# Efficient attention and a mixture of depths on one core: k and v loaded by swapped halves of partitions, their fifth rows multiplied in quarters, the last choice of tokens moved forward, the last product halved, and q of two more units turned on VectorE

## The chip, the cores and the metric

The kernel runs on one core of one Trainium2 chip. A time is the device time of one execution in microseconds (us). A core has TensorE (matrix products, PE in the profile, with its weight loads as PEld), VectorE (DVE), ScalarE (ACT), GpSimd (POOL), SyncE (SP, which issues DMAs), and 16 DMA engines.

## The reference

```python
def _attn_ref(q, k, v):                       # 8 batches, 8 heads, 576 tokens, 64 wide, f32
    q_s = exp(q - max over d);  q_s = q_s / (sum over d + 1e-09)
    k_s = exp(k - max over s);  k_s = k_s / (sum over s + 1e-09)
    kv = np.einsum('bhsd,bhse->bhde', k_s, v)
    return np.einsum('bhsd,bhde->bhse', q_s, kv)

def _moe_ref(x, w_gate, w1, w2, capacity):    # x: (8, 576, 512), capacity 128
    scores = np.einsum('bsd,d->bs', x, w_gate)
    out = x.copy()
    for b in range(B):
        top_idx = np.argpartition(-scores[b], capacity)[:capacity]
        xe = x[b, top_idx]
        ye = np.maximum(xe @ w1, 0.0) @ w2    # w1: 512 x 1024, w2: 1024 x 512
        g = 1.0 / (1.0 + np.exp(-scores[b, top_idx]))
        out[b, top_idx] = x[b, top_idx] + g[:, None] * ye
    return out
```

The attention's heads, side by side, are the x of the second part.

## The kernel before

**Units and steps.** The attention is cut into 16 units of four heads, two units to a batch. A loop over steps `s` (from 3) works on unit `s`, prepares unit `s+1`, loads unit `s+3`, and beside it does one half of the dense products of batch `(s-3)//2`: `mlp1` (x by w1, L591, eight pieces) in odd steps, `mlp2` (by w2, L601, eight pieces) in even ones. The first three units are written out ahead of the loop. The order of instructions on each engine is the order in the text; every engine takes its own in that order and waits by semaphores. `pieces(n)` says how many pieces of the dense products are put at a place.

**A unit.** k, v and q each have three buffers in SBUF, taken in turn. `k_exp` and `v_copy` (ScalarE) make exp(k) and a copy of v with a column of ones. `kv_mm(u)` multiplies them into one PSUM tile `kv`; `kv_out` (DVE) divides by the sums. `q_exp` makes exp(q); `q_t` transposes it on TensorE (L384) and copies it back with ScalarE. For the units in `TWICE`, q is instead loaded in a doubled form of four DMAs, and `q_blocks` transposes it with two DVE instructions (L359). `x_mm` (L414, L405) multiplies q by kv, `x_sums` and `x_scale` (DVE) scale it, `x_store` writes it to `out`.

**Rows of k and v.** A head's 576 tokens are nine rows for each of 64 groups. Two partitions share a group's nine rows: of partitions 2j and 2j+1 the even one holds five rows, the odd one four, for all four heads. `kv_mm` sums five products over 128 partitions. In the fifth the odd partitions hold nothing: k and v are cleared there ahead of the first load of each buffer (`clear`), and the ones column of v is 0 there (`even`, `fifth`). A load is two DMAs, one for the odd partitions (256 elements for each of four heads) and one for the even ones (320).

**Choice of tokens.** After a batch's second unit (odd step), `score` adds up the scores, `score_row` transposes them on TensorE into the `kv` PSUM tile and ScalarE copies them out (`srow`), `compare` counts ranks (five DVE instructions, L493) and `hits` marks which token takes which slot. In the next step `find` turns that into indices (TensorE, L520), `fetch` gathers the rows of `out` (GpSimd, L534), and a step later `turn` transposes them (L571) for `mlp1`. After `mlp2`, `finish` adds gate times product to the rows (DVE, L614) and `put` scatters them (GpSimd, L606). Batch 0's result is kept (`finish_gated`) and written near the end.

**Queues.** SP issues in each step: the store of unit `s`, then k, v and q of unit `s+3`; it takes them in order. The units in `SPREAD` have half of their q issued by GpSimd, early in the step (`odd=True`). From unit 8 on each load's DMA waits for the landing of the one `DEEP` before it.

A fallback for inputs out of range (`general`) follows at the end and isn't entered.

Of the kernel before, what the change touches and what calls it, by code (L numbers as in the profile page):

```python
# [17 lines left out]
def kernel(  # L18
# [23 lines left out]
    nc = tc.nc  # L42
# [58 lines left out]
    LD = 3  # L101
    FLAT = 0, 1
    TWICE = (9, 11, 13, 14, 15)
    SPREAD = TWICE
    RR = 4 * R
# [58 lines left out]
    way = []  # L164
    DEEP = 4
    ROWS = (0, R), (R, T)
# [4 lines left out]

    def clear(u):
        for what in "kv":
            nc.gpsimd.memset(view(raw[what][u % LD], True)[:, :, N2], 0.0)

# [40 lines left out]
    nc.vector.tensor_scalar(valid, second_half, -1.0, 1.0, op0=OP.mult, op1=OP.add)  # L216
    even_p = const.tile([P, 1], I32, name="even_p")
    nc.gpsimd.iota(even_p, pattern=[[0, 1]], base=1, channel_multiplier=1)
    nc.vector.tensor_single_scalar(even_p, even_p, 1, op=OP.bitwise_and)
    even = const.tile([P, 1], F32, name="even")  # L220
    nc.vector.tensor_copy(out=even, in_=even_p)
    beyond = const.tile([P, 1], F32, name="beyond")
# [27 lines left out]
    nc.gpsimd.iota(whole.rearrange("p (b r) -> p b r", b=B), pattern=[[S, B], [1, R]], base=0, channel_multiplier=T)  # L250
    clear(2)
    dma_k = load(1, "k", flat=True)
# [39 lines left out]
    def q_exp(u, c):  # L292
        if c == 0:
            st["qe", u] = at.tile([P, T, 2, D], F32, tag="qe", name="qe")
        if u in TWICE and u not in FLAT:
            half = raw["q"][u % LD].rearrange("p (a n) (h s) -> p a n h s", a=2, h=2)[:, c, :, 0]
            to = st["qe", u].rearrange("p r i d -> p (r i d)").rearrange("p (a n s) -> p a n s", a=2, n=2 * T)
            nc.scalar.activation(out=to[:, c], in_=half, func=AF.Exp)
            return
        r0, r1 = ROWS[c]  # L300
        qr = raw["q"][u % LD][:, :2 * T].rearrange("p (i r) d -> p r i d", i=2)
        nc.scalar.activation(out=st["qe", u][:, r0:r1], in_=qr[:, r0:r1], func=AF.Exp)  # L302

    def v_copy(u, engine=nc.scalar):
# [3 lines left out]
        else:  # L308
            engine.tensor_copy(out=out_v, in_=in_v)

    def fifth(u):
        nc.gpsimd.tensor_copy(out=view(v_ones[u % 2], True)[:, :, N2, D:], in_=even[:, None].to_broadcast([P, 4, 1]))

    def kv_mm(u, crossed=False):
# [16 lines left out]
        for a in range(0 if u in FLAT else 2):  # L333
            for r in range(R):
                for i in range(2):
                    nc.tensor.matmul(out=kv_ps[part(i), a, :D + 1], lhsT=ke[:, 2 * i + a, r], rhs=vo[:, 2 * i + a, r],  # L336
                                     start=(r == 0), stop=(r == N2))
        st["kv", u] = [(slice(0, P), kv_ps[:, :, :D + 1])]
# [54 lines left out]
    def x_mm(u, a, wide=False, tag="x"):  # L393
# [5 lines left out]
        for r in range(R):  # L399
            for i, c in QUARTERS:  # L400
                to = x[part(c), i, r * C:(r + 1) * C]
                if r == N2:
                    if a == 0:
                        rows = by_token[part(i), c, r] if u in TWICE and u not in FLAT else qT[part(i), c, r, 0]
                        last = nc.tensor.matmul(out=to, lhsT=rows, rhs=kw[part(i), c], start=True, stop=True)  # L405
                    continue
                if wide:
# [4 lines left out]
                    continue  # L412
                rows = by_token[part(i), a, R * c + r] if u in TWICE and u not in FLAT else qT[part(i), a, r, c]
                last = nc.tensor.matmul(out=to, lhsT=rows, rhs=kw[part(i), a], start=True, stop=True)  # L414
# [189 lines left out]
    def put(b, n, o):  # L604
# [3 lines left out]
            in_=o[:m], in_offset=None)  # L608

    def finish(b, n):  # L610
        m = slots[n][1]
# [46 lines left out]
    def general():  # L658
        nonlocal FLAT
        FLAT = tuple(range(NU))  # L660
        for n in range(2):
            nc.gpsimd.memset(v_ones[n][:, :, D:], 1.0)
        for b in range(B):
# [79 lines left out]
    x_out(0, 0)  # L743
    clear(3)
    load(3, "kv")
# [10 lines left out]
    x_mm(1, 1)  # L756
    fifth(2)
    x_out(0, 1)
# [11 lines left out]
    q_t(2, 0, wide=True, later=True)  # L770
    clear(4)
    load(4, "kv")
# [13 lines left out]
    k_exp(3)  # L786
    fifth(3)
# [182 lines left out]
```

## Time and profile before

| | |
|---|---|
| median of 3 runs | 208.74 us (208.12 to 213.29) |
| the profiled execution | 209.41 us; its span, first to last instruction, 207.6 us |
| mean granted TensorE clock | 0.986 |
| busy: PE, DVE, ACT, POOL | 193.1, 127.0, 92.1, 40.9 us |
| L591, `mlp1` on PE | 512 instances, 61.8 us |
| L601, `mlp2` on PE | 128 instances, 58.4 us |
| L414, `x_mm` on PE | 960 instances, 22.0 us |
| L336, `kv_mm` on PE | 560 instances, 19.4 us |
| L384, `q_t` on PE | 144 instances, 6.4 us |
| moved by DMA | 49.43 MB, mean 238 GB/s |

An f32 product is listed as two instances, so 20 products are x40. "x" counts instances. A window's DMA share is the mean busy share of the 16 DMA engines; it can exceed 1 where packets overlap. The chain of waits follows back from the last instruction to what released each step; "DMA" in it is the time from an issue to its landing.

### The profile page before, as it was taken

The numbers are of one execution on the slowest core, as the hardware profiler recorded it, in microseconds if no ns is written. First come the engines' busy times: TensorE is split into PE (matmuls) and PEld (weight loads), VectorE is DVE, ScalarE is ACT, GpSimd is POOL, SyncE is SP. The second block draws the span as 40 slices with busy tenths as digits, with TensorE's granted clock in tenths as the row PEclk, the third lists the DMA queues.
The fourth block names the chain that finished last, engine by engine and source line by source line (L and its number), as shares of the span: only waits on it lengthen the run. The fifth ranks groups of instructions, "written<-read, shape, count | busy, mean of one in ns | idle before, by whom it ended". The sixth has DMA issues, their size and how long they took to land.

```text
span 207.6 us, 6693 instructions
## 1 busy us (share of the span) xinstructions
PE 193.1 (93%) x2801; PEld 146.1 (70%) x2801; DVE 127.0 (61%) x392; ACT 92.1 (44%) x136; POOL 40.9 (20%) x110
## 2 busy tenths in 40 slices
PE   7988899999999999999999999999999999999940
PEld 3576788885698749974897569864896479459510
DVE  5776935897278636957684948766696766432010
ACT  4475877673655814772347516452364012111100
POOL 7302100202020403140222132040402030224010
PEclk9999999999999999999999999999999999999995
DMA  6999999999699999899999899999970434031101
GB/s 219 396 294 344 376 363 371 372 374 351 152 295 285 289 356 381 215 296 261 251 285 280 255 230 262 308 269 233 338 210 18 95 114 114 1 102 54 58 17 41
DMA packets 36599, 49.43 MB, mean 238 GB/s; under 512 B 2513, under 2 KB 30673, under 8 KB 36562
## 3 DMA queue, kind: packets, MB, share of 16 engines
q1 hardware_dynamic: 34336, 41.57, 64.8%
q0 software_dynamic: 2080, 7.06, 11.5%
q8 instruction: 24, 0.39, 0.8%
q10 hardware_dynamic: 146, 0.30, 0.5%
q14 instruction: 13, 0.11, 0.1%
HBM read 37.39 MB, written 11.53 MB: 236 GB/s over the span
## 4 chain that ended last, share of the span: by engine, by line
PE 68%; DMA 21%; DVE 2%; issue 2%; ACT 2%; SPq 1%; POOL 1%; POOLq 0%; ACTq 0%
PE mm L591 22%; PE mm L601 21%; DMA k<-in_k_dram 11%; PE x L414 7%; PE kv L336 6%; DMA xr<-out_dram,idx 6%; DMA out_dram<-xs 4%; PE mm L204 3%; PE x L384 2%; PE mm L571 2%; PE kv L479 1%; PE kv L331 1%; PE x L405 1%; PE x L377 1%; DVE xs L439 1%
## 5 line engine op out<-in xcount | busy, mean ns | idle before, releaser
L591 PE MATMUL mm<-xT,w 128*128 128x128 f32 x512 | 61.8, 278 | 0.5 <-DVE xT L579 0.3
L591 PEld LDWEIGHTS mm<-xT,w 128*128 128x128 f32 x512 | 58.7, 192 | 2.3 <-ACT xT L579 1.0
L601 PE MATMUL mm<-w,hT 128*128 128x512 f32 x128 | 58.4, 599 | 0.0
L601 PEld LDWEIGHTS mm<-w,hT 128*128 128x128 f32 x128 | 23.0, 190 | 23.5 <-issue 23.0
L493 DVE SCALAR_TENSOR_TENSOR junk<-srow,s,not_before 128x576 bf16<-128x576 f32 x40 | 32.7, 818 | 5.2 <-ACT srow L485 4.1
L289 ACT ACTIVATE ke<-k 128x1280 f32<-128x1280 f32 (+1 forms) x16 | 20.2, 1260 | 9.8 <-DMA k<-in_k_dram 9.8
L414 PE MATMUL x<-kv_w,qT 64*64 64x66 f32 x960 | 22.0, 222 | 2.1 <-issue 1.4
L439 DVE TENSOR_TENSOR xs<-x,qrec 128x640 f32<-128x640 f32 (+1 forms) x31 | 23.5, 757 | 0.6 <-issue 0.3
L414 PEld LDWEIGHTS x<-kv_w,qT 64*64 64x64 f32 x960 | 18.7, 133 | 5.2 <-issue 4.3
L307 ACT COPY v_ones<-v 128x1280 f32<-128x1280 f32 x14 | 17.6, 1259 | 6.2 <-DMA v<-in_v_dram 6.2
L336 PEld LDWEIGHTS kv<-v_ones,ke 128*64 128x64 f32 x560 | 17.5, 137 | 3.4 <-issue 2.4
L336 PE MATMUL kv<-v_ones,ke 128*64 128x65 f32 x560 | 19.4, 224 | 0.2 <-ACT srow L485 0.2
L614 DVE SCALAR_TENSOR_TENSOR o<-mm,g,xr 128x512 f32<-128x512 f32 x7 | 5.3, 751 | 23.2 <-PE mm L601 23.2
L534 POOL DMA_INDIRECT xr<-out_dram,idx x8 | 8.5, 1061 | 54.6 <-DVE no L526 15.2
L579 ACT COPY xT<-mm 128x512 f32<-128x512 f32 x7 | 4.1, 585 | 31.5 <-PE mm L571 31.5
L606 POOL DMA_INDIRECT out_dram<-o,idx x7 | 7.2, 1026 | 50.5 <-DVE o L614 43.1
L594 ACT ACTIVATE hT<-mm 128x512 f32<-128x512 f32 x16 | 9.5, 596 | 16.5 <-PE mm L591 16.4
L302 ACT ACTIVATE qe<-q 128x640 f32<-128x640 f32 (+1 forms) x22 | 13.9, 677 | 3.5 <-DMA q<-in_q_dram 3.5
L391 ACT COPY qT<-x 128x640 f32<-128x640 f32 (+1 forms) x18 | 10.8, 648 | 9.0 <-PE x L384 8.2
L345 DVE RECIPROCAL krec<-kv 128x2 f32<-128x2 f32 x16 | 2.7, 170 | 18.8 <-PE kv L336 16.4
L431 DVE RECIPROCAL qrec<-x 128x10 f32<-128x10 f32 (+1 forms) x31 | 6.6, 213 | 9.4 <-PE x L405 7.6
L485 ACT ACTIVATE srow<-kv 128x576 f32<-128x576 f32 x7 | 4.5, 648 | 15.2 <-PE kv L479 15.2
(120 smaller groups left out, 187.3 us busy)
## 6 DMA issues: line engine op xcount, KB each, us to landing
out_dram<-xs SPq DMA_DIRECT2D x16, 320.0 KB
k<-in_k_dram SPq DMA_DIRECT2D x14, 320.0 KB
v<-in_v_dram SPq DMA_DIRECT2D x14, 320.0 KB
w<-in_moe_w_dram SPq DMA_DIRECT2D x8, 512.0 KB
out_dram<-xs SPq DMA_DIRECT2D x16, 256.0 KB
k<-in_k_dram SPq DMA_DIRECT2D x14, 256.0 KB
v<-in_v_dram SPq DMA_DIRECT2D x14, 256.0 KB
q<-in_q_dram SPq DMA_DIRECT2D x9, 320.0 KB
```

Source lines behind the costliest of these rows:

```text
L289: nc.scalar.activation(out=ke, in_=view(raw["k"][u % LD], u not in FLAT), func=AF.Exp)
L302: nc.scalar.activation(out=st["qe", u][:, r0:r1], in_=qr[:, r0:r1], func=AF.Exp)
L307: engine.copy(out=out_v, in_=in_v)
L336: nc.tensor.matmul(out=kv_ps[part(i), a, :D + 1], lhsT=ke[:, 2 * i + a, r], rhs=vo[:, 2 * i + a, r], start=(r == 0), stop=(r == N2))
L391: nc.scalar.copy(out=to, in_=src)
L414: last = nc.tensor.matmul(out=to, lhsT=rows, rhs=kw[part(i), a], start=True, stop=True)
L439: nc.vector.tensor_mul(xs[b][:, :n, qd, :, a].rearrange("p r i d -> p i r d"), x[:, :, :, :D], qrec[:, u, a, :, :n].to_broadcast([P, 2, n, ...
L493: nc.vector.scalar_tensor_tensor(junk, st["srow", b], st["s", b][:, r:r + 1], not_before[:, r], op0=OP.subtract, op1=OP.is_ge, accum_out=s ...
L534: nc.gpsimd.indirect_dma_start(out=xr[:m], out_offset=None, in_=out_rows[:(place(b) + 1) * S], in_offset=bass.IndirectOffsetOnAxis(ap=st[" ...
L591: st["piece"] = nc.tensor.matmul(out=h_ps[:, f % 4 * m:(f % 4 + 1) * m], lhsT=w1[:, d, f * P:(f + 1) * P], rhs=xT[:, d, :m], start=(d == 0 ...
L594: nc.scalar.activation(out=hT[:, f - 3:f + 1, :m], in_=h_ps[:, :4 * m].rearrange("p (f c) -> p f c", f=4), func=AF.Relu)
L601: st["piece"] = nc.tensor.matmul(out=st["y", b, n][:m], lhsT=st["hT", b, n][:, f, :m], rhs=w2[:, f], start=(f == 0), stop=(f == KF - 1))
```

## The change

It has five parts. (1) k and v: for two of the four heads (a = 0) partitions 0 to 63 hold rows 0 to 4 of each group and 64 to 127 rows 5 to 8; for the other two it is four rows and five. So the fifth row of head a lies on 64 partitions of its own, and its product is done with those alone, in a quarter of the array, two heads' halves by two. A load is four DMAs of 64 neighbouring partitions and two heads. What is left over in the fifth rows is not used; it is cleared once at the start. (2) q of units 10 and 12 takes the doubled form too. GpSimd issues half of q for units 9 to 13; for 14 and 15 SP issues all four. In steps 10 and 12 two pieces, no longer one, stand ahead of `find`. q of other units from 3 on is one DMA in place of two. (3) `DEEP` is 6. (4) In step 15 `score_row` comes after one piece in place of three; in step 16 `find` comes after one in place of two. (5) The last `mlp2` is done in two halves of 256 columns, each finished and scattered by itself; the loop ends one step sooner.

```diff
-    FLAT = 0, 1
-    TWICE = (9, 11, 13, 14, 15)
-    SPREAD = TWICE
+    FLAT = (0, 1) + ()
+    TWICE = (9, 10, 11, 12, 13, 14, 15)
+    SPREAD = (9, 10, 11, 12, 13)
...
-            if flat:
+            if flat or (u in FLAT and what != "q") or (what == "q" and u not in TWICE and u > 2):
                 t = view(raw[what][u % LD], False)
...
                 t = view(raw[what][u % LD], True)
-                for n, rows in ((1, N2), (0, R)):
-                    dmas.append(nc.sync.dma_start(out=t[n::2, :, :rows].rearrange("p h r d -> p h (r d)"),
-                                                  in_=bass.AP(tensor=src.tensor, offset=first + n * R * D,
-                                                              ap=[[T * D, 64], [SD, 4], [1, rows * D]])))
+                for a in range(2):
+                    for n in range(2):
+                        rows = R if n == a else N2
+                        dmas.append(nc.sync.dma_start(out=t[part(n), a::2, :rows].rearrange("p h r d -> p h (r d)"),
+                                                      in_=bass.AP(tensor=src.tensor,
+                                                                  offset=first + a * SD + n * (T - rows) * D,
+                                                                  ap=[[T * D, 64], [2 * SD, 2], [1, rows * D]])))
...
-    DEEP = 4
+    DEEP = 6
...
         for a in range(0 if u in FLAT else 2):
-            for r in range(R):
+            for r in range(N2):
                 for i in range(2):
                     nc.tensor.matmul(out=kv_ps[part(i), a, :D + 1], lhsT=ke[:, 2 * i + a, r], rhs=vo[:, 2 * i + a, r],
-                                     start=(r == 0), stop=(r == N2))
+                                     start=(r == 0), stop=False)
+        for i, a in QUARTERS if u not in FLAT else ():
+            nc.tensor.matmul(out=kv_ps[part(i), a, :D + 1], lhsT=ke[part(a), 2 * i + a, N2], rhs=vo[part(a), 2 * i + a, N2],
+                             start=False, stop=True)
...
+    def halves(b, n):
+        m = slots[n][1]
+        idx = sl.tile([P, 2], I32, tag="idx_h", name="idx_h", bufs=n_sl)
+        for h in range(2):
+            nc.vector.tensor_scalar(idx[:m, h:h + 1], st["idx", b, n][:m], 2.0, float(h), op0=OP.mult, op1=OP.add)
+        st["idx_h", b, n] = idx
+
+    def last_product(b, n):
...
+        for h in range(2):
+            c = slice(h * half, (h + 1) * half)
+            y_ps = bank("mm", 2)
+            for f in range(KF):
+                nc.tensor.matmul(out=y_ps[:m, :half], lhsT=st["hT", b, n][:, f, :m], rhs=w2[:, f, c],
+                                 start=(f == 0), stop=(f == KF - 1))
+            nc.vector.scalar_tensor_tensor(o[:m, c], y_ps[:m, :half], g[:m], xr[:m, c], op0=OP.mult, op1=OP.add)
+            nc.gpsimd.indirect_dma_start(
+                out=out_halves[:2 * (place(b) + 1) * S],
+                out_offset=bass.IndirectOffsetOnAxis(ap=idx[:m, h:h + 1], axis=0), in_=o[:m, c], in_offset=None)
...
+    LASTP = 1
-    for s in range(LAG, NU + LAG):
+    for s in range(LAG, NU + LAG - 1):
...
-                pieces(1 if here and s not in TWICE else 2)
+                pieces((1 if here and s not in TWICE else 2) if s != NU else LASTP)
                 search()
...
+            if chosen == B - 1:
+                each(halves, chosen)
...
-            pieces(0, to=2 if follows else 3)
+            pieces(0, to=1 if s == NU - 1 else 2 if follows else 3)
...
+    each(last_product, B - 1)
```

Also gone: `even`, `fifth` and the calls of both, and the calls of `clear` for single units; `clear()` now clears all three buffers ahead of the first loads.

More of the change, by code (lines that the diff above doesn't have):

```diff
@@ L170, with clear @@
     load(0, "vq", flat=True)
-    def clear(u):
+    def clear():
         for what in "kv":
-            nc.gpsimd.memset(view(raw[what][u % LD], True)[:, :, N2], 0.0)
+            for n in range(LD):
+                t = view(raw[what][n], True)
+                nc.gpsimd.memset(t[:, :, N2] if n > 1 else t[:, 3:, N2], 0.0)
     w_row = const.tile([1, DM], F32, name="w_row")
@@ L216 @@
     nc.vector.tensor_scalar(valid, second_half, -1.0, 1.0, op0=OP.mult, op1=OP.add)
[L217 to L221, printed above, removed]
     beyond = const.tile([P, 1], F32, name="beyond")
@@ L250 @@
     nc.gpsimd.iota(whole.rearrange("p (b r) -> p b r", b=B), pattern=[[S, B], [1, R]], base=0, channel_multiplier=T)
-    clear(2)
+    clear()
     dma_k = load(1, "k", flat=True)
@@ L294, in q_exp @@
             st["qe", u] = at.tile([P, T, 2, D], F32, tag="qe", name="qe")
-        if u in TWICE and u not in FLAT:
+        if u in TWICE:
             half = raw["q"][u % LD].rearrange("p (a n) (h s) -> p a n h s", a=2, h=2)[:, c, :, 0]
@@ L309, in v_copy @@
             engine.tensor_copy(out=out_v, in_=in_v)
-    def fifth(u):
-        nc.gpsimd.tensor_copy(out=view(v_ones[u % 2], True)[:, :, N2, D:], in_=even[:, None].to_broadcast([P, 4, 1]))
     def kv_mm(u, crossed=False):
@@ L403, in x_mm @@
                     if a == 0:
-                        rows = by_token[part(i), c, r] if u in TWICE and u not in FLAT else qT[part(i), c, r, 0]
+                        rows = by_token[part(i), c, r] if u in TWICE else qT[part(i), c, r, 0]
                         last = nc.tensor.matmul(out=to, lhsT=rows, rhs=kw[part(i), c], start=True, stop=True)
@@ L412, in x_mm @@
                     continue
-                rows = by_token[part(i), a, R * c + r] if u in TWICE and u not in FLAT else qT[part(i), a, r, c]
+                rows = by_token[part(i), a, R * c + r] if u in TWICE else qT[part(i), a, r, c]
                 last = nc.tensor.matmul(out=to, lhsT=rows, rhs=kw[part(i), a], start=True, stop=True)
@@ L608, in put @@
             in_=o[:m], in_offset=None)
+    out_halves = out.rearrange("b s (h d) -> (b s h) d", h=2)
+    def halves(b, n):
[5 more added lines that the diff above has]
+    def last_product(b, n):
+        m = slots[n][1]
+        g, xr, idx = st.pop(("g", b, n)), st.pop(("xr", b, n)), st.pop(("idx_h", b, n))
+        half = DM // 2
+        o = sl.tile([P, DM], F32, tag="o", name="o")
+        for h in range(2):
[8 more added lines that the diff above has]
+                out_offset=bass.IndirectOffsetOnAxis(ap=idx[:m, h:h + 1], axis=0), in_=o[:m, c], in_offset=None)
     def finish(b, n):
@@ L658, in general @@
     def general():
[L659 to L662, printed above, removed]
+        nonlocal FLAT, TWICE
+        FLAT, TWICE = tuple(range(NU)), ()
         for b in range(B):
@@ L743 @@
     x_out(0, 0)
-    clear(3)
     load(3, "kv")
@@ L756 @@
     x_mm(1, 1)
-    fifth(2)
     x_out(0, 1)
@@ L770 @@
     q_t(2, 0, wide=True, later=True)
-    clear(4)
     load(4, "kv")
@@ L786 @@
     k_exp(3)
-    fifth(3)
     v_copy(3)
     LAG = 3
+    LASTP = 1
     AFTER = {4: 2}
```

## The prediction

> **What bounds the kernel now.** I read the page first: busy time by engine and the DMA row of the slices.
>
> ```profile
> PE 193.1 (93%) x2801; PEld 146.1 (70%) x2801; DVE 127.0 (61%) x392; ACT 92.1 (44%) x136; POOL 40.9 (20%) x110
> DMA  6999999999699999899999899999970434031101
> ```
>
> TensorE is busy 193.1 of 207.6 us, and the DMA engines are at nine tenths for three quarters of the span. So time comes from TensorE work taken out, unless a transfer then ends later than its reader wants it. Next I read the chain of waits in order of time, for the places where a transfer does set the pace.
>
> ```profile
> 31.94 7.65 DMA k<-in_k_dram
> 39.69 1.27 ACT ke L289
> 40.96 0.55 ACT srow L485
> 41.55 1.39 PE kv L336 x40
> ...
> 111.61 0.70 PE x L384 x18
> 112.32 1.32 PE kv L336 x40
> ...
> 128.13 7.52 DMA out_dram<-xs
> 136.49 8.73 DMA xr<-out_dram,idx
> 145.27 0.66 PE mm L571 x4
> ...
> 183.47 0.64 PE mm L571 x4
> 192.81 6.88 PE mm L601 x16
> 199.72 0.76 DVE o L614
> 201.03 0.69 POOL out_dram L606
> ```
>
> Columns: start, length, what. There are two such places. At 39.6 us k of unit 5 lands, `k_exp(5)` runs at once, `srow` behind it on ScalarE, and `kv_mm(4)` waits for `srow`: a later k is paid in full. At 128 to 145 us the store of unit 11's rows takes 7.5 us to land and the gather behind it 8.7 us, and `turn` of batch 5 (L571) starts with it. Elsewhere the chain is TensorE's own. The tail is one product of 6.88 us, an element-wise instruction, and a scatter. Last the stretches, for what the DMA engines move per share of busy time:
>
> ```profile
> core 0: us, PE busy (x) PEld busy (x) DVE busy (x) ACT busy (x) POOL busy (x), PEclk, DMA share, GB/s
> 14.00:40.00 26.00, 23.63 (x450) 20.77 (x449) 17.50 (x58) 18.14 (x31) 2.31 (x12) 1.00 1.05 358
> 118.00:156.00 38.00, 37.19 (x531) 29.39 (x530) 27.04 (x75) 16.39 (x23) 8.06 (x21) 1.00 0.94 256
> 164.00:178.00 14.00, 13.50 (x154) 11.08 (x153) 9.10 (x23) 2.43 (x4) 2.32 (x8) 1.00 0.42 104
> ```
>
> Loads early run at 358/1.05 = 341 GB/s of a full share; the late mix at 256/0.94 = 272; stores nearly alone at 104/0.42 = 248. The stores read 64 neighbouring partitions at a time, the shape that the k and v loads are given.
>
> **The change, part by part.** The profiled execution took 209.41 us (span 207.6, 1.8 around it); it stands 0.67 above the median, 208.74. The sum is made on 209.41.
>
> 1. *q of units 10 and 12 twice.* `q_t(10)` and `q_t(12)` go, 18 transposes each: 0.70 us in the chain at 111.61, the same form at 133.67 in TensorE's timeline. -1.40. What comes instead: four DVE transposes of 0.76 (group L359), 3.0 us. In step 9 the first fits into the 0.70 that DVE waits for `srow` before its ranks at 106.00, the second into the 2.25 idle before `kv_out` at 114.32. `hits` comes some 0.1 later, but `find` in steps 10 and 12 is put one more piece (0.86, from 6.88/8) back, so it doesn't wait; with that cover gone it would be 0.76 a step. ScalarE loses 2 x 1.18 us of copies. The two q loads grow from 576 to 1120 KB, 0.56 MB each: 2.1 us at 272 GB/s, ahead of the saturated stretch; see 5.
>
> 2. *Fifth rows in quarters.* Of 40 instances (1.32 us, 33 ns each) 32 stay; 8 become 64x64 quarters. The 64x64 kv product at the start (L331) does 72 in 1.21 us, 17 ns each. So 0.27 us become 0.13: 0.13 a unit, 14 units, 1.8 us. Two corrections. Units 2 and 3 lie before the k of 39.6 us and save nothing: 12 units, 1.56. And a change of tile shape isn't free: the first 32 instances of `x_mm`, after a wider tile, take 0.63 and the second 32, alike, 0.47 (57.24 and 57.98 in the chain), so 0.16. For units 7, 9, 11, 13, 15 `x_mm` follows at once and that cost only moves; for the other 7 it is new. So 5 x 0.13 plus 7 x (between -0.03 and 0.13): 0.4 to 1.6; I take 1.0, since some of the 0.16 is the load of first weights, which a stream already running hides. -1.0. The Trainium skill (TensorEngine Tiling, Key Properties) speaks against this edit: a change of tiling mode drains the array. By that rule the seven units give nothing and the term is 0.4; the row of 0.16 agrees in kind, and whether it is all drain no row shows.
>
> 3. *Last choice sooner.* `score_row(7)` comes after one piece instead of three in step 15, `find(7)` after one instead of two in step 16. DVE now waits 1.47 us for `srow` before the ranks at 173.25; its x_scale ends at 171.78, so ranks and `hits` can come 1.4 sooner, and `find` 0.86. The gather then lands 0.86 sooner against `turn`, whose wait on it is 0.32 (183.47). -0.3; bounds 0 and 0.32. The 0.15 wait for xT at 185.11 stays. The halved indices (two DVE instructions of about 0.15, as L525) fall into DVE's 5.2 us idle after 179.8.
>
> 4. *Last product halved.* 16 products of 256 columns for 8 of 512: by columns the same 6.88 (0.43 halved is 0.215 an instance; on a line through the 128-column instances, 5.36/48 = 0.11, it is 0.218, 0.1 us in all against). DVE's last instruction falls from 0.76 to between 0.42 (a 256-column copy, L731) and 0.76; I take 0.47. The scatter still writes 128 rows, 1.0 to issue (L606), with half the bytes to land (scatters landed in 2.8 to 6.9 us); the first half is issued 3.4 us earlier and is gone by then. -0.28 and about -0.15: -0.45; bounds +0.1 and -0.8.
>
> 5. *Order of loads.* The odd halves of q(14) and q(15) leave GpSimd's queue, where q(14)'s went out at 123.64 ahead of unit 11's store and q(15)'s at 137.6 beside the gather, and go behind k and v on SP. That takes 573 KB, 2.1 us at 272 GB/s, from before the store and as much from beside the gather and k, v of unit 15. Against it: TensorE comes about 2 us sooner, and q(12) adds 2.1 us just before. I let these cancel and take only the wait at 145.27 (0.30) as gone: -0.3; bounds -0.3 and +2.5.
>
> 6. *k and v in four DMAs of 64 partitions.* The same bytes and packet sizes, twice the issues. An issue of v takes 0.60 on SP (L152, least), of w 0.37, so 3.0 to 4.8 us a unit for 2.4. In a step SP has that time free (nothing is issued from 112.2 to 118.3), and x+0 goes first; q behind them goes 0.6 to 2.4 later and has a step to land. Before 39.6 us it has not: SP there waits for landings (a k load issued at 16.19 lands at 23.88, the next issue is at 23.95), with seven k or v tensors ahead. If the new shape moves at the rate of the loads, the cost is small; at the stores' rate the 1.18 MB of a unit take 4.76 us for 3.46, and 3.5 units make 4.5 us, all paid at `kv_mm(4)`. Bounds 0 and +4.5. I take +0.3, nearer the loads, because now too each DMA serves 64 partitions, and direction and packets stay. The Trainium skill (DMA: Bandwidth & Descriptors, Rules for kernel authors) is against this split: two transfers to disjoint halves serialize on the same 16 engines, one of 128 partitions is to be used. That alone leaves the engines' time as it is and would make only the issues dearer.
>
> The cleared rows, `fifth` and `even` (GpSimd memsets 0.3 to 0.7 us, L174) go or move to the start; GpSimd is at 20% and nobody waits for them.
>
> Sum: -1.40 -1.0 -0.3 -0.45 -0.3 +0.3 = -3.15. 209.41 - 3.15 = 206.26 in the profiled execution's terms, **205.6** as a median.
>
> **Rivals.**
>
> *Loads in halves are slow (slower than before).* Place: 14 to 40 us, then 118 to 156. Price: 4.5 at `kv_mm(4)`; for units 13 to 15 3 x 1.3 less the 1.8 us that v(15) has now (copied by 155.9, used at 157.67), 2.1; and q(12)'s 2.1 no longer absorbed. 8.7 against a gain of 3.45 from the rest: +5.25, 214.0. It turns the sign from 3.45 on, and passes 2% from 7.6. For it: stores at 248 GB/s of a share. Against: stores write to HBM; loads don't.
>
> *Hidden anyway.* The store and gather before 145.27 pace that stretch by bytes, so q_t and the kv gains ahead of it become a longer wait at L571. Left: 0.3 + 0.45, two kv units (0.26), a little of 5: 1.1, 207.6. For it: a share of 0.94, and the 0.30 wait already there. Against: only 0.30, and part 5 relieves just this place.
>
> *All of it, and more.* kv at its full 1.8, choice 0.32, tail 0.8, wait 0.3, and the three stops of 0.38 in `x_mm` after 145 us ("issue") go with fewer instructions and calmer queues: 1.4 + 1.8 + 0.32 + 0.8 + 0.3 + 1.1 = 5.7: 203.0. Against: nothing shows what those stops wait for.
>
> **How the numbers follow.** The forecast 0.43 (own range 204.4 to 206.9), slow halves 0.17, hidden 0.20, all 0.20. 2%, about what a measurement of this kernel can tell from no change (its three times lie 2.5% apart), is 204.57 and 212.9. Faster by over 2%: 0.17 of the last rival and 0.17 of the forecast, 0.34. Slower: 0.13 of the slow halves. Within: 0.53. The range goes from 202.6 to 211.0, which leaves out some 0.07 of the last rival and 0.13 of the slow halves.
>
> **What would show it.** Right: no L384 in steps 10 and 12; kv of units 7, 9, 11 in about 1.19 us; L571 near 143 and 181 without a wait; a last DVE instruction near 0.47; k(5) landing by 40 us. Wrong: k(5) past 41 with `kv_mm(4)` waiting as long; DMA share over 1 and GB/s down in 14 to 40 us; L571 of batch 5 waiting over 1 us; kv units at 1.3 or more.

## The result, and the profile after

The changed kernel takes 223.5 us (median of 6 runs, 221.03 to 225.4) against 208.81 (6 runs): a ratio of 1.0674, 95% interval 1.0595 to 1.0754, some 14 us slower. Some executions of any of these kernels fall into a slower state of the chip, at a lower clock; the medians count all runs, the ratios leave those out. The profiled execution took 224.14 us, span 222.4, mean granted clock 0.954.

From its page, the busy line of TensorE, the DMA row and the row of the granted clock:

```profile
PE 197.4 (89%) x2781; PEld 152.7 (69%) x2781; DVE 130.2 (59%) x397; ACT 90.7 (41%) x132; POOL 39.3 (18%) x108
PEclk9999996785999999999699999999999999999996
DMA  6989989999897889999998999997999462331110
```

Twenty instances fewer, but TensorE is busy 4.3 us longer: in slices 7 to 10 (33 to 56 us) and 20 (106 to 111) its clock fell. Where it stood still before that is in its timeline (start, length, instruction, and in brackets the idle time and what ended it):

```profile
35.92 1.22 PE L384 MATMUL x<-ident,qe 64*128 64x64 f32 x18 [3.56 <-ACT qe L302]
37.07 2.00 PE L333 MATMUL kv<-v_ones,ke 128*64 128x65 f32 x32
39.00 0.49 PE L336 MATMUL kv<-v_ones,ke 64*64 64x65 f32 x8
...
50.10 2.00 PE L333 MATMUL kv<-v_ones,ke 128*64 128x65 f32 x32 [4.44 <-ACT srow L485]
```

`q_t(3)` waits 3.56 us for q of unit 3, `kv_mm(4)` 4.44 us for k of unit 5 (by way of `k_exp(5)` and `srow`). ScalarE's timeline has that landing; in the kernel before, `k_exp(5)` starts at 39.69:

```profile
48.23 1.27 ACT L289 ACTIVATE ke<-k 128x1280 f32<-128x1280 f32 x1 [5.93 <-DMA k<-in_k_dram]
```

Behind each wait the products take nearly twice as long (2.00 for 1.15): the granted clock is 0.50 from 37 to 41 us and from 50 to 55. In the chain of waits (start, length, what) the early loads lead up to both, v of unit 9 to the stop at 103 us, and the tail is its own:

```profile
28.23 6.88 DMA q<-in_q_dram
...
37.68 8.35 DMA q<-in_q_dram
46.05 3.77 DMA v<-in_v_dram
49.85 0.21 ACT srow L485
50.10 2.00 PE kv L333 x32
...
67.36 1.08 PE kv L333 x32
68.44 0.28 PE kv L336 x8
...
95.21 8.09 DMA v<-in_v_dram
103.40 1.26 ACT v_ones L307
104.65 0.51 ACT hT L594
...
207.51 6.92 PE mm L628 x32
214.46 0.49 DVE o L630
```

At full clock (67.36) a unit's kv is 1.08 + 0.28 = 1.36 us, where 1.19 was forecast and 1.32 stood before; what the quarters give behind them is taken up under *m_quarters*. In the queue of SP, a tensor is 2.69 and 3.43 us of issuing, and k of unit 5 goes out from 38.27 us (the last line has three of its four DMAs, since its window ends at 40 us):

```profile
9.06 2.69 SPq L154 DMA_DIRECT2D k<-in_k_dram  x4
11.87 3.43 SPq L154 DMA_DIRECT2D v<-in_v_dram  x4
...
38.27 2.12 SPq L154 DMA_DIRECT2D k<-in_k_dram  x3
```

The kernel before took 1.47 for the two DMAs of the first of these, and issued k of unit 5 from 31.09:

```profile
9.70 1.47 SPq L152 DMA_DIRECT2D k<-in_k_dram  x2
...
31.09 1.45 SPq L152 DMA_DIRECT2D k<-in_k_dram  x2
```

Last, the stretch 14 to 40 us (columns: PE, PEld, DVE, ACT, POOL busy, clock, DMA share, GB/s):

```profile
14.00:40.00 26.00, 21.12 (x355) 18.45 (x353) 14.49 (x43) 16.90 (x28) 1.32 (x7) 0.90 0.93 259
```

Before it was a share of 1.05 and 358 GB/s. Both numbers fell: the DMA engines had gaps, and moved less while busy, 259/0.93 = 278 GB/s of a full share for 341. These are two causes, and the experiments take them apart.

### The profile page after: what moved, and what is told of

It is laid out like the page before. It is cut to its first block, busy times and chain, and to the rows that moved or that the text cites. A ratio compares the mean times of both kernels' runs of the same rounds, so it can differ in the third digit from the quotient of the medians.

```text
span 222.4 us, 6732 instructions
## 1 busy us (share of the span) xinstructions
PE 197.4 (89%) x2781; PEld 152.7 (69%) x2781; DVE 130.2 (59%) x397; ACT 90.7 (41%) x132; POOL 39.3 (18%) x108
## 4 chain that ended last, share of the span: by engine, by line
PE 63%; DMA 22%; SPq 6%; ACT 3%; issue 2%; DVE 1%; POOL 0%; POOLq 0%; ACTq 0%
PE mm L591 21%; PE mm L601 19%; DMA k<-in_k_dram 7%; DMA q<-in_q_dram 7%; PE kv L333 6%; PE x L414 6%; DMA v<-in_v_dram 5%; SPq L154 3%; DMA xr<-out_dram,idx 3%; PE mm L628 3%; PE mm L571 2%; PE x L384 2%; PE kv L336 2%; PE kv L479 1%; SPq L192 1%
## 5 line engine op out<-in xcount | busy, mean ns | idle before, releaser
L591 PE MATMUL mm<-xT,w 128*128 128x128 f32 x512 | 63.6, 282 | 0.3 <-DVE xT L579 0.3
L591 PEld LDWEIGHTS mm<-xT,w 128*128 128x128 f32 x512 | 60.3, 196 | 2.1 <-ACT xT L579 0.7
L601 PE MATMUL mm<-w,hT 128*128 128x512 f32 x112 | 51.4, 600 | 1.7 <-ACT hT L594 1.7
L601 PEld LDWEIGHTS mm<-w,hT 128*128 128x128 f32 x112 | 20.1, 190 | 21.9 <-issue 19.6
L333 PEld LDWEIGHTS kv<-v_ones,ke 128*64 128x64 f32 x448 | 16.6, 156 | 8.0 <-ACT srow L485 4.6
L302 ACT ACTIVATE qe<-q 128x640 f32<-128x640 f32 (+1 forms) x18 | 11.4, 674 | 6.9 <-DMA q<-in_q_dram 6.9
L606 POOL DMA_INDIRECT out_dram<-o,idx x6 | 6.2, 1028 | 37.8 <-DVE o L639 32.0
L639 DVE SCALAR_TENSOR_TENSOR o<-mm,g,xr 128x512 f32<-128x512 f32 x6 | 4.5, 750 | 13.2 <-PE mm L601 13.2
L463 POOL TENSOR_TENSOR s<-s_all,valid_r 128x5 f32<-128x5 f32 x8 | 1.6, 194 | 57.1 <-DVE s_all L461 57.1
L391 ACT COPY qT<-x 128x640 f32<-128x640 f32 (+1 forms) x14 | 8.4, 648 | 5.0 <-PE x L384 3.5
```

The costliest lines, as they stand in the source:

```text
L391: nc.scalar.copy(out=to, in_=src)
L591: st["piece"] = nc.tensor.matmul(out=h_ps[:, f % 4 * m:(f % 4 + 1) * m], lhsT=w1[:, d, f * P:(f + 1) * P], rhs=xT[:, d, :m], start=(d == 0 ...
L601: st["piece"] = nc.tensor.matmul(out=st["y", b, n][:m], lhsT=st["hT", b, n][:, f, :m], rhs=w2[:, f], start=(f == 0), stop=(f == KF - 1))
```

## The experiments

Ratios are to the kernel before, run on the same chip. It took between 205.2 and 209.0 us as a median from chip to chip, so kernels of different groups are compared by ratio. All columns but the median and the ratio come from one profiled execution of each kernel. "k(5)" is the start of `k_exp(5)` in ScalarE's timeline, which can't come before k of unit 5 has landed; "wait" is that of `kv_mm(4)`; the last columns are the stretch 14 to 40 us.

| kernel | median us | ratio (95%) | k(5) | wait | share | GB/s | GB/s of a full share |
|---|---|---|---|---|---|---|---|
| before | 208.81 | 1 | 39.69 | 0.17 | 1.05 | 358 | 341 |
| changed | 223.5 | 1.0674 (1.0595 to 1.0754) | 48.23 | 4.44 | 0.93 | 259 | 278 |
| c_issues | 223.03 | 1.0701 (1.0642 to 1.0761) | 45.29 | 4.69 | 0.87 | 280 | 322 |
| d_halves | 223.76 | 1.0736 (1.0681 to 1.079) | 50.40 | 5.85 | 1.09 | 261 | 239 |
| b_rest | 208.9 | 1.001 (0.9944 to 1.0077) | 40.18 | 2.37 | 1.02 | 352 | 345 |
| e_two_queues | 217.06 | 1.0587 (1.0441 to 1.0733) | 41.03 | 0.48 | 1.04 | 357 | 343 |
| h_mixed | 209.89 | 1.0187 (1.0073 to 1.0301) | 39.89 | 1.93 | 1.04 | 356 | 342 |
| f_fill | 220.07 | 1.0725 (1.0648 to 1.0802) | 48.69 | 1.57 | 0.94 | 246 | 262 |
| j_two_halves | 231.8 | none; 1.10 by two runs | 55.06 | 4.62 | 1.07 | 266 | 249 |
| k_order_rest | 206.86 | 0.9875 (0.9824 to 0.9926) | 37.81 | 0 | 1.02 | 353 | 346 |
| l_order_before | 207.85 | 0.9951 (0.9923 to 0.998) | 36.92 | 0 | 1.05 | 359 | 342 |

**One cause at a time: issues, halves, and the rest.** Four kernels ran on one chip.

*c_issues*: the kernel before, four DMAs a tensor, still every other partition.

```diff
-                for n, rows in ((1, N2), (0, R)):
-                    dmas.append(nc.sync.dma_start(out=t[n::2, :, :rows]...
+                for a in range(2):
+                    for n, rows in ((1, N2), (0, R)):
+                        dmas.append(nc.sync.dma_start(out=t[n::2, a::2, :rows]...
...
-    DEEP = 4
+    DEEP = 6
```

> The kernel before, with each load of k and v cut into four DMAs of two heads (DEEP 6), on every other partition as before: the number of issues of the changed kernel, without its neighbouring partitions. Theory 'issues': what made the changed kernel slow is that SP takes 0.60 us for each of twice as many DMAs and has only eight of them, half as large, in flight; then the waits at 36 and 50 us (3.6 and 4.4 us, and the slow clock behind them) come back and the time is 216 to 222 us. Theory 'halves': it is the 64 neighbouring partitions, which the DMA engines serve more slowly; then this one has no such wait and takes 208 to 211 us.

*d_halves*: the kernel before, two DMAs a tensor, of partitions 0 to 63 and 64 to 127.

```diff
-                    dmas.append(nc.sync.dma_start(out=t[n::2, :, :rows]...
+                    dmas.append(nc.sync.dma_start(out=t[part(n), :, :rows]...
...
-        nc.gpsimd.tensor_copy(out=..., in_=even[:, None]...
+        nc.gpsimd.tensor_copy(out=..., in_=valid[:, None]...
```

> The kernel before, with two DMAs for each k and v as before, but of partitions 0 to 63 and 64 to 127 in place of every other one; products as before, the empty fifth rows now on 64 to 127. Theory 'issues': as before, 207 to 210 us. Theory 'halves': k of unit 5 lands several us after 39.6, kv_mm(4) waits for it, and the time is 215 to 222 us; DMA share near 1 with fewer GB/s from 14 to 40 us.

*b_rest*: the change without its k and v part (loads, products and `DEEP` as before).

> The changed kernel with k and v loaded and multiplied as before (two DMAs, every other partition, five products, DEEP 4); kept are q of 10 and 12 twice, the sooner choice, the halved last product. Both theories on k and v: 205.5 to 207.5 us, which is 208.8 less 1.4 for q_t, 0.3 for the choice and 0.45 for the tail. A third theory, that q of 10 and 12 in doubled form overloads the DMA engines: 209 us or more, with waits near v(10) and xr at 100 to 140 us.

*a_kv*: the k and v part with `TWICE`, `SPREAD` and the loads of q as before.

> The changed kernel with q loaded as before (TWICE 9, 11, 13, 14, 15, all of them half by GpSimd, q in two DMAs). Theory that k and v alone made it slow: 221 to 225 us, since the waits at 36 and 50 us stay. Theory that the doubled q has a good part in it: 216 to 219 us, with the wait of 3.3 us near 103 us gone.

Each of the two causes alone costs the whole loss. The stretch 14 to 40 us, first of c_issues, then of d_halves, shows that they are different ones:

```profile
14.00:40.00 26.00, 22.54 (x443) 20.00 (x442) 16.23 (x52) 17.81 (x30) 2.31 (x10) 1.00 0.87 280
```

```profile
14.00:40.00 26.00, 20.50 (x364) 18.02 (x363) 14.80 (x43) 16.63 (x28) 1.95 (x10) 1.00 1.09 261
```

In c_issues the DMA engines are fed too slowly (share 0.87) and serve nearly as well as before (322 GB/s of a full share). In d_halves they are always busy (1.09) and serve at 239. My two theories were put as rivals; both hold.

For "fed too slowly" there is another candidate than the price of an issue. In these traces SP has at most eight DMAs under way: in the kernel before, the issue at 23.95 us is the eighth after that of 16.19 and follows its landing at 23.88. Eight DMAs half as large are half the bytes. But from 14 to 40 us SP waited some 8.5 us for landings in the kernel before and 1.2 us in c_issues, so there its own issues are the bound. In the changed kernel, with slow halves as well, it waited 6.2.

a_kv takes 223.59 us, by a single run. As far as one run can, it says that the k and v part alone makes the loss, not the doubled q; b_rest says the same from the other side: it neither loses nor gains (1.001, 0.9944 to 1.0077). In its profiled execution TensorE comes earlier to `kv_mm(4)` and waits there.

```profile
42.04 1.39 PE L338 MATMUL kv<-v_ones,ke 128*64 128x65 f32 x40 [2.37 <-ACT srow L487]
```

**The loads by themselves.** *bench_loads* has no work but loads, in seven stretches. The loop, cut:

```python
    for shape in ("every_other", "half", "every_other_four", "half_four", "all", "half_two_queues", "every_other"):
        for n in range(6):
            load(shape, n)                                  # 590 KB of k or v
        nc.vector.memset(raw[:, :, 0:2 * R, 0:1], 0.0)      # the next stretch waits for this
```

> The loads alone, with nothing computed (the output isn't the reference's): six k or v tensors of 590 KB, 3.54 MB, in each of seven stretches one after the other, each stretch waiting for the one before: (1) two DMAs of every other partition, as the kernel before; (2) two DMAs of partitions 0 to 63 and 64 to 127; (3) four of every other partition; (4) four of neighbouring halves, as the changed kernel; (5) one DMA of all 128 partitions; (6) as 2, one half issued by SP and the other by ScalarE; (7) as 1 again. Theory 'two causes' (each DMA costs SP 0.60 to 0.65 us, and 64 neighbouring partitions at a time are served slower): 1, 5 and 7 at 330 to 350 GB/s, 10.1 to 10.7 us of transfer; 2 at 225 to 265, 13.4 to 15.7 us at a full share; 3 bound by 24 issues of 0.65, 15.6 us, 227 GB/s at a share of 0.7; 4 no faster than the slower of both. For 6, if the slowness is that one half alone is written at a time, over 300 GB/s; if each packet to such a half is slow, as 2. Rival 'only beside other work' (the shapes differ only when TensorE, ScalarE and VectorE work on the same memory, or when other loads are mixed in): all of 1, 2, 5 and 7 within 10% of each other.

VectorE's timeline, where the idle time ahead of each memset is the length of a stretch:

```profile
23.22 0.11 DVE L118 MEMSET raw<- 128x60 f32 x1 [14.36 <-DMA raw<-in_v_dram]
41.54 0.11 DVE L118 MEMSET raw<- 128x60 f32 x1 [18.21 <-DMA raw<-in_v_dram]
59.65 0.11 DVE L118 MEMSET raw<- 128x60 f32 x1 [18.00 <-DMA raw<-in_v_dram]
77.85 0.11 DVE L118 MEMSET raw<- 128x60 f32 x1 [18.10 <-DMA raw<-in_v_dram]
90.38 0.11 DVE L118 MEMSET raw<- 128x60 f32 x1 [12.42 <-DMA raw<-in_v_dram]
108.04 0.11 DVE L118 MEMSET raw<- 128x60 f32 x1 [17.55 <-DMA raw<-in_v_dram]
122.14 0.11 DVE L118 MEMSET raw<- 128x60 f32 x1 [14.00 <-DMA raw<-in_v_dram]
```

And windows inside the first four, the fifth and the sixth (DVE, POOL busy, clock, share, GB/s):

```profile
13.00:21.00 8.00, 0.00 (x0) 0.00 (x0) 1.00 0.98 324
28.00:40.00 12.00, 0.00 (x0) 0.00 (x0) 1.00 1.10 228
46.00:57.00 11.00, 0.00 (x0) 0.00 (x0) 1.00 0.79 228
64.00:75.00 11.00, 0.00 (x0) 0.00 (x0) 1.00 0.82 231
82.00:90.00 8.00, 0.00 (x0) 0.00 (x0) 1.00 0.90 324
96.00:107.00 11.00, 0.00 (x0) 0.00 (x0) 1.00 1.10 237
```

The first and the last stretch, two every-other DMAs, take 14.36 and 14.00 us. With nothing computed, the same bytes take 18.21 us in neighbouring halves, 18.00 in four every-other DMAs, and 18.10 with both: the two costs don't add up, the larger decides, and here they happen to be alike. That answers why the kernel with both is no slower than those with one. The rival "only beside other work" is out. Halves on two queues (sixth) are little better than on one, 17.55. The queue of SP shows the price of an issue in the fourth and fifth stretch:

```profile
59.78 2.56 SPq L89 DMA_DIRECT2D raw<-in_k_dram  x4
...
77.99 0.41 SPq L110 DMA_DIRECT2D raw<-in_k_dram  x1
```

A DMA of 64 partitions takes 0.64 us whether it carries four heads (1.28 for two) or two (2.56 for four); one of 128 partitions and all the bytes takes 0.4. So halving a DMA doubles the price of a byte, and 147 KB each 0.65 us can be no more than 226 GB/s: stretch 3 moved 228, its 24 DMAs issued one behind the other. The Trainium skill (DMA: Bandwidth & Descriptors, Rules for kernel authors) says that transfers to disjoint partition halves serialize, from one queue or two, and to use one of 128 partitions: stretches 2, 6 and 5 agree (18.21, 17.55, 12.42). The measurement adds that it matters which half: 64 neighbouring partitions are served at 228 GB/s, 64 alternate ones at 324, with the same reads from DRAM. Why is not shown.

**Undoing one cause.** *e_two_queues* is c_issues with half of the early issues taken from SP; *j_two_halves* is the changed kernel with half of its early issues taken from SP.

```diff
+                queue = nc.gpsimd if what == "v" and u < 6 else nc.sync        # e_two_queues
...
+                        queue = nc.gpsimd if n and u < 6 else nc.sync          # j_two_halves
```

> The kernel before with each k and v load in four DMAs on every other partition, as in c_issues (223.03), but the four DMAs of v of units 2 to 5 are issued by GpSimd; everything else stays on SP. Theory 'issues' (each DMA costs SP 0.60 us, so twice as many hold k of unit 5 back): k and v are then issued side by side, k(5) lands by 41 us instead of 45.2, the wait of 4.69 us at kv_mm(4) and the half clock behind it go, and 215 to 218 us remain, the rest of c_issues' loss being paid after 100 us. Rival 'smaller transfers' (the DMA engines serve 128 descriptors a transfer worse than 256, whoever issues them): k(5) lands at 44 us or later, 222 to 224 us.

> The changed kernel, but of each k and v load of units 2 to 5 the two DMAs of partitions 64 to 127 are issued by GpSimd and the two of partitions 0 to 63 by SP. Theory 'two causes': SP has half the issues, and the halves are moved side by side instead of one after the other, so k(5) lands by 42 us, and the time is h_mixed's, 1.02 times the kernel before or 211 to 214 us. Rival 'halves stay slow' (the service of a half is slow whatever moves beside it): k(5) at 45 to 50 us, a ratio of 1.05 to 1.07, 218 to 223 us.

e_two_queues brings the loads back to 357 GB/s and k(5) to 41.03, the wait to 0.48. So the issues held the early loads back there, not the smaller transfers. The time came back less than I expected: 1.0587 is 221 on a kernel of 208.8, and its interval (1.0441 to 1.0733) overlaps that of c_issues, so the gain is shown in the loads and the wait, not in the time. TensorE now stops 2.02 us at 16 us for kv_out, and 1.60, 2.10 and 1.35 after 80 us for v and hT; its late k and v loads are still four DMAs each on SP. j_two_halves is worse than the changed kernel by two runs (231.29 and 227.94), beyond both expectations: the DMA engines have no gap (1.07) but serve at 249, which confirms slow halves; and k(5) comes still later, 55.06. Why later was not tried; SP, with fewer issues ahead of them, hands q and the matrices to the DMA engines sooner, so k may share them with more.

**How much is early.** *h_mixed* is the changed kernel with k and v of units 2 to 5 loaded and multiplied as before.

```diff
+                for n, rows in ((1, N2), (0, R)) if u < EARLY else ():     # EARLY = 6
+                    dmas.append(nc.sync.dma_start(out=t[n::2, :, :rows]...
-                for a in range(2):
+                for a in range(2 if u >= EARLY else 0):
```

> The changed kernel with k and v of units 2 to 5 loaded and multiplied as before (two DMAs of every other partition, five whole products a head) and of units 6 to 15 as changed (four DMAs of neighbouring halves, quarters). Theory 'paid early': the waits of 3.56 us at q_t(3) and 4.44 us at kv_mm(4) go with the half clock behind them (5.1 us), 223.5 - 13.1 = 210.4, and what is left over 208.4 is the two waits for hT at 102 to 105 us: 209.5 to 211.5. Rival 'paid everywhere' (the late loads cost as much as soon as the early ones don't stop TensorE): 214 to 218. Rival 'late gain' (late loads hide, the other parts of the change bring their 2 us): 206 to 207.5.

1.0674 becomes 1.0187 (1.0073 to 1.0301): 4.9% of 208.8, 10.2 us, are early; 3.9 us are late, each give or take some 2.5. On a kernel of 208.8 it would be 212.7, between "paid early" and "paid everywhere", nearer the first. The late part is three stops behind k and v, in TensorE's timeline:

```profile
78.96 1.15 PE L348 MATMUL kv<-v_ones,ke 128*64 128x65 f32 x32 [1.31 <-ACT v_ones L315]
...
93.22 0.27 PE L535 MATMUL mm<-vals,hit 128*128 128x5 bf16 x5 [1.19 <-ACT hT L609]
...
105.21 1.15 PE L348 MATMUL kv<-v_ones,ke 128*64 128x65 f32 x32 [1.85 <-ACT v_ones L315]
```

At the first, v of unit 8 has just landed. At the second, `hT` stands on ScalarE behind `k_exp(9)`, which waited 3.21 us for k, and `v_copy(9)`. At the third, `v_copy(10)` comes late (103.89 us) with no releaser shown; the last DMA of v of unit 10 was issued at 96.44. 4.35 us in all.

**Is the half clock part of the price?** *f_fill* puts idle products where TensorE waits.

```diff
+            fill(10)
             q_t(3, 0)
...
+            fill(14)
             kv_mm(4)
```

> The changed kernel with 24 matmuls more that compute nothing that is used: ten before q_t(3) and fourteen before kv_mm(4), 0.21 us each, which run where TensorE stood still for 3.56 and 4.44 us. Theory 'half clock' (part of the loss isn't waiting but TensorE at half clock after a long wait): the two stretches of 6.8 us at clock 0.5 go; the one at 36 us saves nothing, since kv_mm(4) waits for k(5) all the same and waits longer; the one at 50 us gives back 1.13 in kv_mm(4), 1.0 in the eight L591 and 0.4 in q_t and kv_mm(5), so 2.5 us: 220.5 to 221.5. Rival 'transfers set the pace anyway': the 2.5 us come back as waits for loads at 100 us, 223 to 224.

The products ran in the gaps, the two early stretches at half clock went (2.00 is 1.15 again at 50 us), and the ratio is that of the changed kernel, 1.0725 and 1.0674 with overlapping intervals. My 2.5 us didn't come. The faster stretch ended in other stops: at 60 us TensorE stood 1.85 us with no releaser shown, and half clock followed there. The half clock is seen, but these runs don't show that taking it away gives time.

**Where the gains were.** *g_tail*: the kernel before with the last choice sooner and the last product halved.

> The kernel before with two parts of the change alone: the last choice sooner and the last product in halves (q of units 9, 11, 13, 14, 15 twice and the k and v loads and products as before). By the prediction's terms 3 and 4, -0.3 and -0.45: 207.4 to 207.9. Rival 'no gain' (b_rest showed none, at 208.9): 208.2 to 208.8.

0.9987 (0.9948 to 1.0026): undecided between the two. Its TensorE, too, waited at `kv_mm(4)`, 1.50 us. So I moved the load that stands ahead of k(5):

```diff
     load(4, "kv")
-    load_w2(0)
     load(4, "q")
     load(5, "kv")
+    load_w2(0)
     load_w2(1)
```

*k_order_rest* is b_rest with it, *l_order_before* the kernel before with it.

> b_rest (the change without its k and v part; 1.001 times the kernel before) with one line moved: the first half of the second expert matrix, 0.5 MB, is loaded behind k and v of unit 5 instead of ahead of q of unit 4. Theory 'hidden at kv_mm(4)' (b_rest's TensorE came 2 us sooner and then waited 2.37 us for k(5)): k(5) lands about 1.5 us sooner, the wait shrinks to about 1, and the gain comes through: a ratio of 0.990 to 0.995, 206.3 to 207.4. Rival 'the matrix is then late' (its first products are at 46 us and now wait): 1.00 or more, 208.5 to 210.

> The kernel before with the same line moved and nothing else. There kv_mm(4) waits 0.2 us or less, so a k(5) that lands 1.5 us sooner finds no wait to shorten: ratio 0.998 to 1.002. If it is under 0.995, the early loads bound the kernel before too, and part of what k_order_rest shows is the order alone.

k_order_rest is faster than both kernels, 0.9875 (0.9824 to 0.9926), a little past the expected range: no wait at `kv_mm(4)`, and the matrix isn't late. For l_order_before I was wrong: 0.9951 is no zero. Its TensorE came to `kv_mm(4)` at 39.64 us, 1.9 sooner than in the profiled execution before, and found k there (`k_exp(5)` at 36.92); in the old order, with k at 39.69, it would have waited. The profiled executions bear that out. In the old order `kv_mm(4)` starts at 41.55 to 42.44 us whether `kv_mm(3)` came late (34.71, before) or early (33.01 in b_rest, 33.15 in h_mixed, 34.26 in g_tail); in the new one it starts 6.6 us behind `kv_mm(3)`, at 39.64 to 41.19, in all five kernels that have it. So the line moved lets an early start count.

It does not explain why b_rest alone gained nothing, since what b_rest saves lies behind `kv_mm(4)`. From `kv_mm(6)` to the end its profiled execution takes 207.2 - 55.75 = 151.45 us, the kernel before 207.6 - 55.26 = 152.34. b_rest has six stops in `x_mm` there with no releaser shown, 2.45 us, and the kernel before three, 1.14. Those stops are 1.3 us more than before, and ahead of `kv_mm(6)` only 0.5 us is lost; what they wait for stays open. Then the single terms:

*m_quarters* (k_order_rest with the changed `kv_mm`), *n_tail_order* (l_order_before with terms 3 and 4), *o_twice_order* (l_order_before with the new `TWICE` and `SPREAD`).

> k_order_rest (0.9875 times the kernel before), with the products of k and v as in the changed kernel: 32 of 128 rows and 8 quarters a unit; loads as in the kernel before. In this layout the quarters leave out half of the fifth tokens and the result differs; the instructions and their operands' shapes are those of the changed kernel. By the prediction's term 2, -1.0 us against k_order_rest: a ratio of 0.980 to 0.985. Rival 'the change of shape drains what the quarters save' (1.08 and 0.28 in the trace of the changed kernel for 1.32 before, so 12 units at 0.04 more each): 0.987 to 0.992, no gain.

> l_order_before (the kernel before with the second matrix's first half behind k and v of unit 5; 0.9951) and on it terms 3 and 4 alone: the last choice sooner, the last product in halves. With the early loads out of the way these are paid in full if the prediction's -0.75 holds: a ratio of 0.990 to 0.993. If the tail gives nothing: 0.994 to 0.997.

> l_order_before and on it term 1 alone: q of units 10 and 12 loaded twice and transposed by VectorE, the odd halves of 14 and 15 on SP. Predicted -1.4 with another -0.3 of term 5: a ratio of 0.987 to 0.990. If VectorE or the bytes of these loads take it back: 0.994 or more.

m_quarters: 0.9905 (0.9865 to 0.9946) against 0.9875: no gain, with no load in the way.

```profile
66.94 1.15 PE L338 MATMUL kv<-v_ones,ke 128*64 128x65 f32 x32
68.02 0.34 PE L341 MATMUL kv<-v_ones,ke 64*64 64x65 f32 x8
68.19 0.65 PE L419 MATMUL x<-kv_w,qT 64*64 64x66 f32 x32
68.66 0.30 PE L410 MATMUL x<-kv_w,qT 64*64 64x66 f32 x8
```

And a unit of k_order_rest, with whole products and the same loads:

```profile
156.82 1.39 PE L338 MATMUL kv<-v_ones,ke 128*64 128x65 f32 x40
158.14 0.70 PE L416 MATMUL x<-kv_w,qT 64*64 64x66 f32 x32
158.66 0.30 PE L407 MATMUL x<-kv_w,qT 64*64 64x66 f32 x8
```

The eight quarters begin 1.08 us after the whole products. Where `x_mm`, of the same tile shape, follows at once, it starts 0.17 us later, and its first 32 take 0.47 for 0.52: from the start of kv, 68.66 - 66.94 = 1.72 us for 158.66 - 156.82 = 1.84, a gain of 0.12 in five units. Where products of 128x128 follow, they start 0.28 us after the first quarter: 1.36 for 1.32, a loss of 0.04 in seven units. By the trace the quarters so give 0.3 us, less than the times can tell from nothing.

n_tail_order: 0.9914 (0.9881 to 0.9947), 0.8 us less than l_order_before. o_twice_order: 0.9909 (0.9874 to 0.9945), 0.9 us less, half of what I gave it. Its trace shows four waits of `turn` for the gather, 0.78, 0.48, 0.28 and 0.16 us, where the kernel before has two, 0.30 and 0.32. (In b_rest and k_order_rest, with the same loads of q, `turn` doesn't wait at all, so they are not the rule.) Two of them:

```profile
121.58 0.66 PE L571 MATMUL mm<-ident,xr 128*128 128x128 f32 x4 [0.78 <-DMA xr<-out_dram,idx]
...
142.87 0.66 PE L571 MATMUL mm<-ident,xr 128*128 128x128 f32 x4 [0.48 <-DMA xr<-out_dram,idx]
```

The intervals overlap that of l_order_before (0.9923 to 0.998), so neither 0.8 nor 0.9 is clear of noise by itself. 0.9914 x 0.9909 / 0.9951 = 0.987 is k_order_rest's ratio: the two together would make it.

## Why the prediction was wrong

I said 205.6; it is 223.5. Point by point, by its own steps:

- **Term 6, the four DMAs, +0.3 (bounds 0 and +4.5): the step that failed.** It is about 14 us: 10.2 early, 3.9 late, each give or take some 2.5, and b_rest shows that the rest of the change adds no loss. Three things in it were wrong. *The issues.* I had 0.60 us an issue and "3.0 to 4.8 us a unit", and beside it 3.46 us for a unit's bytes at the loads' rate, but did not set the one against the other: with eight issues a unit, SP, not the DMA engines, is what limits the early loads. I found SP's free time in a late step, wrote that before 39.6 us it has none, and still called the cost small if the shape moves at the loads' rate. I also misread the row for it: between the issues of 16.19 and 23.95 us SP didn't stand still, it issued seven DMAs and then waited for the one of 16.19, eight back, to land. c_issues is this error alone, +14.6 us. *The halves.* I took the loads' rate because "now too each DMA serves 64 partitions". Which 64 matters: 239 GB/s of a full share for neighbours, 341 for every other. The stores' rate, 248, was the right row, and I used it only for the bound. d_halves is this error alone, +15.4. *The place.* I let the delay be paid once, at `kv_mm(4)`. k(5) came 8.5 us later, so the delay alone was nearly double the bound, and q(3) was paid 3.56 us ahead of it. Late loads were paid again: 1.66 and 1.63 us of stops at 102 to 105 us, behind k and v of unit 9.
- **The rival of slow halves, 214.0.** Right in sign, in the place 14 to 40 us and in the row that spoke for it; too small, since it counted one cause, 3.5 units, and a gain of 3.45 from the rest that b_rest does not show. My chance of 0.17 for it was too low: the row of the stores and the rule on halves both pointed to it, and against them stood only that loads don't write to HBM.
- **Term 2, quarters, -1.0: 0.3 by the trace of m_quarters, and nothing that its times show** (0.9905 against 0.9875). Five units gain 0.12, the 0.13 I had; seven lose 0.04, the worst end of my -0.03 to 0.13. I priced those quarters by the row of 17 ns, where 72 come in a row, and hoped that a running stream hides part of the change of shape; eight that stand between two other shapes take 0.28, and it hides nothing. The Trainium skill (TensorEngine Tiling (Array Packing), Key Properties) states that a change of tiling mode drains the array. The 0.4 that I worked out by that rule (with the seven units at -0.03; at nothing it would be 0.65) is near the 0.3.
- **Term 1, q twice, -1.4 (and 5, -0.3): half, not clear of noise.** The 36 instances of L384 are gone, and o_twice_order shows 0.9 us, beside 1.7 us of waits of `turn` for the gather (0.6 before). In that execution it is the rival "hidden anyway", whose place I had at 145 us; b_rest and k_order_rest have no such wait. In the changed kernel the wait at batch 5's `turn` is 0.75, not gone.
- **Terms 3 and 4, -0.75: about right in n_tail_order (0.8), not clear of noise;** g_tail, in the old order, showed 0.3. `turn` of the last batch no longer waits (198.64 in the chain of the changed kernel follows its neighbour at once), and the last instruction of VectorE is 0.49 for the 0.47 I took. But from the start of the last product to the end it is 222.4 - 207.51 = 14.9 us, and before 207.6 - 192.81 = 14.8: what VectorE saves, the last scatter's landing keeps. So the 0.8 is not shown to come from the tail.
- **The k of 39.6 us.** I had seen the place and said that a later k is paid in full, but not that an execution which starts earlier is held there too: b_rest waits 2.37 us for k(5) where the kernel before waits 0.17. That place can't have taken the rest's gains, which lie behind it; why b_rest alone shows none stays open, with its longer stops in `x_mm` as the nearest row.

## What to carry to other kernels

Before cutting a load into more DMAs, set the issue time per byte beside the DMA engines' time per byte: here 0.65 us for 147 KB is 226 GB/s, under the 341 that the engines did, and the queue became the bound. Keep a DMA spread over all partitions, and take the rate of its shape from the row that has that shape, even if that row is a store. Where a load is what a stretch waits for, time saved ahead of it shows only once that load comes sooner: one line moved gave 0.5% by itself. With the rest of the change it gave 1.2%; that the rest alone gave nothing is not explained by that load.

## What the runs showed of the hardware

- An issue on SP costs 0.64 us for a DMA of 64 partitions with four runs each or with two, and 0.4 for 128 partitions with two runs each.
- With four runs to a partition, 64 neighbouring partitions are loaded at 228 GB/s with all DMA engines busy (share 1.10), 64 alternate ones at 324 (0.98), in packets of the same sizes and with nothing else running.
- The two costs overlap: 18.21 us, 18.00 us, and 18.10 with both.
- `x_mm`, 72 short products in about 1.1 us, has stops of 0.37 to 0.46 us with no releaser: three in the kernel before, six in b_rest (2.5 us), none in g_tail, n_tail_order, o_twice_order and m_quarters. These four ran on chips where the kernel before takes 205.2 us, the first two where it takes 208.4 to 208.8, so the chip may matter more than the kernel; what the stops wait for stays open.
